# Squared-relu attention and a Fourier mixing layer on one core: blocks of 128 keys instead of 112, other groups of tokens, and a planned order without single corrections

## The chip, the cores and the metric

The kernel runs on one core of a Trainium2 chip. Its metric is the time on the device in microseconds, from one launch; fewer is better. TensorE multiplies matrices, VectorE (DVE) and ScalarE (ACT) do elementwise work, GpSimd (POOL) does some of it and issues the loads that change the type, and SyncE (SP) issues the other transfers, DMA transposes among them.

## The reference

```python
# q, k, v: (8, 12, 448, 64) float32; w_ch1: (768, 3072); w_ch2: (3072, 768)
scores = q @ k.T / sqrt(64)
attn = maximum(scores, 0) ** 2 / 448
x = attn @ v                      # heads side by side: (8, 448, 768)
mixed = real(fft(fft(x, axis=1), axis=2))
u = x + mixed
un = (u - mean(u)) / sqrt(var(u) + 1e-6)
out = u + maximum(un @ w_ch1, 0) @ w_ch2
```

There is no softmax: a block of keys contributes its squared relu times its values, and contributions add up.

## The kernel before

The whole program is written out by a planner (`Streams`) before it runs. Each piece of work is a Python generator that asks for an engine with `need(engine, duration, dependencies, buffers)`; the planner starts, over and over, the piece that could start first by its own estimates, and that fixes the order of instructions on every engine. Engines are strictly in order, so a late operand holds up all that stands behind it. Two tables correct the estimates: `HEAD` moves all pieces of a kind in a phase, and `NUDGE` (line 71) moves one step of one piece. Constants such as `LEAD` (how far attention runs ahead of the feed-forward part) and the margins added to a load's expected landing belong to the same plan.

**Attention.** A batch has 12 heads in three groups of four, a group has two pairs of heads. `load_group` brings q, k and v of a group with one DMA each, with four consecutive tokens on one of 112 partitions: 448 = 112 x 4. For the first two batches `turn_on_pe` transposes q and k on TensorE; later VectorE reorders them (`qkr`, line 539) and a DMA transposes them (`qkT`, line 551). An item of work is one block of 112 keys for a pair of heads: two matmuls of scores (`score`, line 888), each on one half of the array's rows, so that the two run together; a relu on ScalarE out of PSUM (`squares`, line 901); a square on VectorE or ScalarE (`square`, lines 918 and 915); and two matmuls with the values (lines 816 and 873), which again share the array. A pair of heads has four items, a batch 24. After the first batch TensorE visits attention between pieces of the feed-forward part, for up to three items of scores and the values of one pair.

**Mixing.** `fold` and `halves` use the symmetry of the Fourier transform, `mix` multiplies along channels (line 1383), `mix_rows` along tokens, adds x, and normalizes to `un`. Rows of `un` go to DRAM and come back transposed (`turns`), but the first batch and most of the second are turned on TensorE (`turn_rows`, line 1139).

**Feed-forward.** It works on groups of tokens, whose bounds are `GT`: 384, 384 and then eleven of 256. The first layer is line 1870, its relu line 1857. In the second layer a block of 128 tokens is either a whole or half of a `Pair`. A pair (256 tokens, line 2008) needs 84 matmuls of 384 columns where two plain blocks would need 96; it uses sums of weights (`weight_sums`) and sums of hidden blocks made on VectorE. The first group's blocks are plain (line 1898), the second group has a pair and a whole (line 1923), the later ones a pair each. The last four groups are done two at a time (`joint`), with a similar saving in the first layer too.

**Loads.** GpSimd issues them in the order of `loading`: batch 0, q and k of two groups of batch 1, the first weights (`load_w1`), values, then the second weights (`load_w2`) between the groups that follow. For the first three batches at most eight are under way (`ring`).

Of the kernel before, what the change touches and what calls it, by code (L numbers as in the profile page):

```python
# [10 lines left out]
FP32 = mybir.dt.float32  # L11
BF16 = mybir.dt.bfloat16
# [29 lines left out]
class Banks(Bufs):  # L42
# [28 lines left out]
NUDGE = {  # L71
# [6 lines left out]
}  # L78
# [6 lines left out]
class Streams:  # L85
    def __init__(self):
        self.engine = dict.fromkeys(LATENCY, 0.0)
        self.streams = []
        self.fill = lambda: False
        self.port = 0.0  # L90
        self.dma_free = {"sw": 0.0, "hw": 0.0}
        self.count = {}

    def add(self, gen, rank):
        name = gen.gi_code.co_name
        self.count[name] = self.count.get(name, 0) + 1
        self.streams.append([gen, rank, None, name, f"{name}.{self.count[name]}", 0])
# [20 lines left out]
    def run(self):  # L118
        end = {}
        while self.streams:  # L120
            for s in self.streams:
                if s[2] is None:
                    try:
                        s[2] = s[0].send(end.pop(id(s), None))
                        s[5] += 1
# [6 lines left out]
            for s in self.streams:  # L132
# [8 lines left out]
                key = (ok is not None and not ok(), max(t) + HEAD.get((s[3], eng, phase), 0.0) + NUDGE.get((s[4], s[5]), 0.0), s[1][eng != "PE"])  # L141
# [53 lines left out]
def kernel(  # L195
# [34 lines left out]
    WHOLE, FOURTH = 3, 0.1  # L230
    JOINTS = list(range(9, NGR, 2))
# [26 lines left out]
    zero_t = const.tile([128, 1], FP32, name="zero_t")  # L258
    eps_t = const.tile([128, 1], FP32, name="eps_t")
    halfpi = const.tile([128, 1], FP32, name="halfpi")  # L260
# [4 lines left out]
    back = [const.tile([128, 1], mybir.dt.int32, name=f"back{i}") for i in range(2)]  # L265
    back2 = [const.tile([128, 1], mybir.dt.int32, name=f"backe{i}") for i in range(2)]
# [20 lines left out]
    def small_constants():  # L287
# [3 lines left out]
        nc.vector.memset(warm, 0.0)  # L291

    def pads():
        for x in xTc:
# [120 lines left out]
    TURNED, STORED, RELAYED = 1.1055, 1.0, 0.0  # L415
# [13 lines left out]
    def load_group(i, which=(0, 1, 2)):  # L429
# [3 lines left out]
        for x, (nm, src) in enumerate((("q", q), ("k", k), ("v", v))):  # L433
            if x not in which:
                continue
            if b == 0 and x < 2:
                e = yield need("POOL", 0.75, ring())
                t = first_qk[x][:R, g]
            else:
                e = yield need("POOL", 0.75, ring() if b < 3 else [], [BQ[x] if x == 2 else BQ[x][home(i)]])  # L440
                t = work.tile([R, HG, 4 * Dh], BF16, name=f"{nm}n",
                              tag="vn" if x == 2 else f"{nm}n{home(i)}", bufs=3 if x == 2 else 1)
# [1704 lines left out]
```

## Time and profile before

| | us |
|---|---|
| median of 3 runs | 577.06 |
| the runs | 573.18, 577.06, 578.73 |
| the profiled execution, its own time | 574.73 |
| span of that execution in the trace | 572.7 |
| TensorE busy in it | 559.8 |
| VectorE / ScalarE / GpSimd busy | 446.3 / 341.7 / 143.4 |

Groups of instructions are given by line, engine and tile, with their count, the time that they cover and the mean of one in ns. Matmuls overlap: their mean is the time of one from its start to its drain, and the time from start to start is shorter. Timeline rows give the start, the time covered and, in brackets, the idle time before and what ended it. The table of stretches gives, for each, its length, the busy time of each engine with its number of instructions, the clock that TensorE was granted, the busy share of the DMA engines (all queues added up) and the bytes moved.

### The profile page before, as it was taken

The numbers are of one execution on the slowest core, as the hardware profiler recorded it, in microseconds if no ns is written. First come the engines' busy times: TensorE is split into PE (matmuls) and PEld (weight loads), VectorE is DVE, ScalarE is ACT, GpSimd is POOL, SyncE is SP. The second block draws the span as 40 slices with busy tenths as digits, with TensorE's granted clock in tenths as the row PEclk, the third lists the DMA queues.
The fourth block names the chain that finished last, engine by engine and source line by source line (L and its number), as shares of the span: only waits on it lengthen the run. The fifth ranks groups of instructions, "written<-read, shape, count | busy, mean of one in ns | idle before, by whom it ended". The sixth has DMA issues, their size and how long they took to land.

```text
span 572.7 us, 11611 instructions
## 1 busy us (share of the span) xinstructions
PE 559.8 (98%) x4434; PEld 366.5 (64%) x4434; DVE 446.3 (78%) x1030; ACT 341.7 (60%) x573; POOL 143.4 (25%) x193
## 2 busy tenths in 40 slices
PE   8999999899999999999999999999999999999997
PEld 6466556454655846746756756756768688668864
DVE  6988773999797488998998789889899747544843
ACT  5978772789785556877786667748616054106400
POOL 8537101421150111542443225124033000000000
PEclk9999999999999999999999999999999999999999
DMA  9999999697874989599999879934255330322012
GB/s 125 206 211 252 191 225 152 209 133 124 155 181 127 183 103 163 155 177 199 215 158 183 161 124 193 215 106 138 71 131 181 76 104 7 91 96 85 1 44 94
DMA packets 134404, 82.25 MB, mean 144 GB/s; under 512 B 78365, under 2 KB 129566, under 8 KB 134350
## 3 DMA queue, kind: packets, MB, share of 16 engines
q0 software_dynamic: 40384, 33.82, 38.6%
q1 hardware_dynamic: 93966, 47.70, 36.2%
q8 instruction: 34, 0.56, 0.4%
q14 instruction: 20, 0.16, 0.1%
HBM read 62.91 MB, written 26.45 MB: 156 GB/s over the span
## 4 chain that ended last, share of the span: by engine, by line
PE 83%; DVE 8%; DMA 4%; ACT 3%; issue 1%; POOL 1%; DVEq 0%; POOLq 0%; ACTq 0%
PE psF L1870 24%; PE psF L2008 22%; PE psS L1704 7%; PE psS L2008 7%; PE psS L888 6%; PE psF L816 4%; PE psF L1898 3%; PE psF L1704 2%; DMA qkT<-qkr 2%; PE psS L1383 2%; ACT sq L901 2%; DVE sq L918 2%; DMA qk<-in_k_dram 2%; PE psF L1923 1%; PE psS L816 1%
## 5 line engine op out<-in xcount | busy, mean ns | idle before, releaser
L901 ACT ACTIVATE sq<-psS 112x896 bf16<-112x896 f32 x192 | 164.8, 924 | 44.1 <-PE psS L888 43.7
L1870 PE MATMUL psF<-unT,w 128*128 128x256 bf16 (+1 forms) x1296 | 165.8, 285 | 1.0 <-ACT hT L1857 0.7
L1870 PEld LDWEIGHTS <-w 128*128 128x128 bf16 x1296 | 123.6, 98 | 42.4 <-issue 10.8
L918 DVE TENSOR_TENSOR sq<-sq 112x896 bf16<-112x896 bf16 x160 | 98.6, 636 | 9.6 <-ACT sq L901 8.9
L2008 PEld LDWEIGHTS <-hT 128*128 128x128 bf16 x720 | 68.8, 98 | 49.8 <-issue 6.6
L1857 ACT ACTIVATE hT<-psF 128x512 bf16<-128x512 f32 (+3 forms) x136 | 66.2, 504 | 37.9 <-PE psF L1870 37.1
L2008 PE MATMUL psF<-w,hT 128*128 128x384 bf16 x378 | 67.1, 326 | 0.0
L888 PE MATMUL psS<-qkT 64*128 64x448 bf16 (+1 forms) x384 | 52.8, 358 | 3.4 <-DVE qs L1191 1.9
L1568 DVE TENSOR_TENSOR o<-psF,o 128x384 f32<-128x384 f32 x72 | 39.7, 551 | 14.3 <-PE psF L2008 12.6
L888 PEld LDWEIGHTS <-qkT 64*128 64x128 bf16 (+1 forms) x384 | 16.8, 101 | 31.8 <-issue 22.2
L1719 ACT COPY copies<-psS 128x256 f32<-128x256 f32 x51 | 17.8, 374 | 29.0 <-PE psS L1704 26.3
L443 POOL DMA_DIRECT2D qn<-in_q_dram x21 | 15.5, 736 | 73.4 <-DVE qkr L539 73.0
L816 PE MATMUL psF<-sq,vn 112*64 112x448 bf16 x264 | 31.6, 358 | 1.0 <-DVE sq L918 1.0
L443 POOL DMA_DIRECT2D vn<-in_v_dram x24 | 17.3, 722 | 57.6 <-PE psS L888 38.4
L1704 PEld LDWEIGHTS <-w 128*128 128x128 bf16 x288 | 28.1, 98 | 4.3 <-issue 0.2
L1209 POOL TENSOR_TENSOR u<-tp,xn 112x385 f32<-112x385 f32 (+2 forms) x14 | 14.7, 1051 | 62.4 <-DVE tp L1189 60.1
L915 ACT ACTIVATE sq<-sq 112x896 bf16<-112x896 bf16 x32 | 30.1, 955 | 0.3
L642 DVE TENSOR_SCALAR xT<-psF 128x224 bf16<-128x224 f32 x56 | 19.1, 382 | 13.3 <-PE psF L816 13.2
L1218 DVE BATCH_NORM_STATS2 stats<-u 112x6 f32<-112x384 f32 (+2 forms) x56 | 29.1, 545 | 0.3 <-POOL u L1211 0.3
L2008 PE MATMUL psF<-wsum,hT 128*128 128x384 bf16 x162 | 29.0, 326 | 0.0
L816 PEld LDWEIGHTS <-vn 112*64 112x64 bf16 x336 | 15.7, 109 | 19.1 <-issue 12.6
L1568 DVE TENSOR_TENSOR o<-psS,o 128x384 f32<-128x384 f32 x21 | 11.6, 556 | 20.2 <-PE psS L2008 20.2
(233 smaller groups left out, 887.8 us busy)
## 6 DMA issues: line engine op xcount, KB each, us to landing
out_dram<-o SPq DMA_DIRECT2D x56, 192.0 KB, 2.1
vn<-in_v_dram POOLq DMA_DIRECT2D x24, 224.0 KB, 5.8
qn<-in_q_dram POOLq DMA_DIRECT2D x21, 224.0 KB, 5.2
kn<-in_k_dram POOLq DMA_DIRECT2D x21, 224.0 KB, 7.0
w<-in_moe_w_ch_dram POOLq DMA_DIRECT2D x12, 384.0 KB, 13.5
w<-in_moe_w_ch_dram POOLq DMA_DIRECT2D x4, 1152.0 KB, 19.6
utop<-u SPq DMA_DIRECT2D x12, 336.0 KB, 3.1
o<-utop SPq DMA_DIRECT2D x16, 192.0 KB, 5.3
```

Source lines behind the costliest of these rows:

```text
L443: nc.gpsimd.dma_start(out=t, in_=src[b, hs].rearrange("h (p j) d -> p h (j d)", j=4))
L816: nc.tensor.matmul(av[h * Dh:(h + 1) * Dh, 0:S], lhsT=vn[:, c, h0 + h, :], rhs=sq[:, h, :], start=(c == 0), stop=(c == 3))
L888: nc.tensor.matmul(sc[:wide, h, 0:S].rearrange("k (c q) -> k c q", c=4), lhsT=flat[ps, k0:k0 + wide], rhs=qT[ps, m % 2], start=True, stop= ...
L901: nc.scalar.activation(r, sc[:R, :, 0:S], AF.Relu)
L915: nc.scalar.activation(r, r, AF.Square)
L918: nc.vector.tensor_tensor(r, r, r, op=ALU.mult)
L1218: nc.vector.bn_stats(stats[:n, hf, :], u[:n, hf * (D // 2):(hf + 1) * (D // 2)])
L1568: nc.vector.tensor_tensor(o, pc[:, 0:DH], o, op=ALU.add)
L1704: nc.tensor.matmul(ps[:, 0:N], lhsT=lhs, rhs=rhs[:, m], start=(start and m == 0), stop=(stop and m == 2), skip_group_check=True)
L1857: nc.scalar.activation(hs, ps, AF.Relu)
L1870: nc.tensor.matmul(ph[:, i * N:(i + 1) * N], lhsT=w1_sb[m][hf][:, (jj + i) * 128:(jj + i + 1) * 128], rhs=unT[:, m, 0:N], start=(m == 0), ...
L2008: nc.tensor.matmul(pc[:, 0:DH], lhsT=lhs[i], rhs=rhs[i], start=(start and i == 0), stop=(i == KP - 1), skip_group_check=True)
```

## The change

Keys are loaded so that 384 of the 448 of a head lie on 128 partitions, three to each; the last 64 keys of two heads share a fourth block, one head on partitions 0 to 63 and the other on 64 to 127, beside zeros that are written once into homes that stay for k (`kn_homes`) and v (`vn_home`). So a group has seven items for its two pairs instead of eight: six with 128 keys for two heads, and one shared item (`r == 3`), whose two score matmuls use the whole array, one for each pair, and whose values take one matmul for each pair. `load_halves` brings the last 64 keys with two DMAs. The groups of tokens become 384, 512, 384 and nine of 256: the second has a pair and two wholes, the third a pair and a whole, and the fourth weight sum is formed twice. All of batch 1's `un` is now turned on TensorE, and `part_store` goes. The second weights' first quarter is loaded later. `NUDGE` goes with its counting, `HEAD` keeps two entries, and some constants of the plan change. Small tiles (constants, statistics) are put together into larger ones. The cut diff:

```diff
-HEAD = {
-    ('attentions', 'PE', 2): -0.6, ('attentions', 'PE', 3): -0.619, ('chain_b', 'PE', 2): 0.232,
-    ('early', 'DVE', 3): -0.057, ('first', 'DVE', 4): -0.122, ('halves', 'DVE', 1): 0.209,
-    ('halves', 'DVE', 2): -0.148, ('late', 'DVE', 4): -0.128, ('outputs', 'SP', 1): -2.572,
-    ('turn_x', 'SP', 1): 2.085, ('turn_x', 'SP', 2): 0.783, ('turn_x', 'SP', 3): 0.049, ('turns', 'SP', 3): -0.991,
-}
-NUDGE = {
-    ('attentions.1', 45): 0.8, ('attentions.1', 48): 0.28, ('chain_a.1', 4): 0.28, ('chain_a.1', 8): 0.8,
-    ('chain_a.10', 4): -0.13, ('chain_a.11', 8): 0.26, ('chain_b.3', 2): -1.86, ('ffns.1', 123): 0.3,
-    ('ffns.1', 5): -0.53, ('ffns.1', 76): 0.8, ('halves.1', 3): 0.77, ('leave.37', 1): 0.3, ('main.24', 3): -0.3,
-    ('main.7', 6): 0.5, ('mix_rows.7', 3): -1.5, ('rows.12', 4): 0.3, ('rows.14', 3): -0.3, ('rows.23', 2): 1.5,
-    ('rows.9', 2): -1.5, ('squares.75', 1): 0.8, ('third.11', 2): -0.38, ('third.12', 2): -0.8,
-    ('turning.2', 18): 0.26, ('turning.2', 43): 1.7,
-}
+HEAD = {('attentions', 'PE', 2): -0.6, ('attentions', 'PE', 3): -0.6}
...
                 t = [self.engine[eng]] + [d.t if isinstance(d, Cell) else d for d in deps]
                 for p in set(bufs):
                     t.append(sorted(p.free)[bufs.count(p) - 1])
-                key = (ok is not None and not ok(), max(t) + HEAD.get((s[3], eng, phase), 0.0) + NUDGE.get((s[4], s[5]), 0.0), s[1][eng != "PE"])
+                key = (ok is not None and not ok(), max(t) + HEAD.get((s[3], eng, phase), 0.0), s[1][eng != "PE"])
...
+    KB, KT = 128, 3 * 128
+    NB = 7 * NG
...
-    GT = [0, 384] + list(range(768, B * S + 1, 256))
+    GT = [0, 384, 896] + list(range(1280, B * S + 1, 256))
...
-    WHOLE, FOURTH = 3, 0.1
-    JOINTS = list(range(9, NGR, 2))
+    WHOLE = 3
+    JOINTS = list(range(8, NGR, 2))
...
+        clear(nc.vector, first_qk[1].rearrange("p g h x -> p (g h) x")[:, :, 3 * Dh:])
+        clear(nc.vector, vn_home[:, 3 * H * Dh:].rearrange("p (h d) -> p h d", d=Dh))
 
     def pads():
+        for t in kn_homes:
+            clear(nc.gpsimd, t[:, :, 3 * Dh:])
...
+    arrived = {}
+
+    def arrive(i, x):
+
+        arrived.setdefault((i, x), []).append(landed[-1])
+        if len(arrived[i, x]) == (1, 2, 2)[x]:
+            ready[i][x].t = max(arrived[i, x]) + (1.5 if i % NG else 0.0, 3.0, 6.0, 8.0)[min(i // NG, 3)]
+
+    def load_halves(b, g, n, x):
+
+        if b == 0 and x == 1:
+            t = first_qk[1].rearrange("p g h x -> p (g h) x")[:, :, 3 * Dh:]
+        elif x == 1:
+            t = kn_homes[home(b * NG + g)][:, :, 3 * Dh:]
+        else:
+            t = vn_home[:, (3 * H + g * HG) * Dh:(3 * H + (g + n) * HG) * Dh].rearrange("p (h d) -> p h d", d=Dh)
+        for par in range(2):
+            e = yield need("POOL", 0.75, ring() if b < 3 else [])
+            at = (k, v)[x - 1][b, g * HG + par:(g + n) * HG:2, KT:].rearrange("h p d -> p h d")
+            nc.gpsimd.dma_start(out=t[par * Dh:(par + 1) * Dh, par::2], in_=at)
+            landed.append(sch.dma(e, n * HG * Dh * Dh * 2, 390e3, "sw"))
+        for i in range(g, g + n):
+            arrive(b * NG + i, x)
+
+    def load_group(i, which=(0, 1, 2), parts=(0, 1)):
...
+                if x == 0:
+                    to, j, rows = t, 4, S
+                else:
+                    to, j, rows = (t[:, :, 0:3 * Dh] if x == 1 else
+                                   t.rearrange("p (h x) -> p h x", h=HG)), 3, KT
+                nc.gpsimd.dma_start(out=to, in_=src[b, hs, 0:rows].rearrange("h (p j) d -> p h (j d)", j=j))
+                loads[i][x] = None if x == 2 else t.rearrange("p h (j d) -> p j h d", j=4)
+                landed.append(sch.dma(e, GRP * rows / S, 390e3, "sw"))
+                arrive(i, x)
...
+            if x and 1 in parts and (b > 0 or g == x - 1):
+                yield from load_halves(b, g if b else 0, 1 if b else NG, x)
...
+    kn_homes = [work.tile([128, HG, 4 * Dh], BF16, name="kn", tag=f"kn{i}", bufs=1) for i in range(QN)]
+    vn_home = work.tile([128, H * 4 * Dh], BF16, name="vn", tag="vn", bufs=1)
+
+    def clear(eng, t):
+
+        for n in range(2):
+            eng.memset(t[n * Dh:(n + 1) * Dh, 1 - n::2], 0.0)
...
-        yield from load_group(NG, (0, 1))
-        yield from load_group(NG + 1, (0, 1))
+        yield from load_group(NG, (0, 1), (0,))
+        yield from load_group(NG + 1, (0, 1), (0,))
         yield from load_w1(0)
+        yield from load_group(NG, (1,), (1,))
+        yield from load_group(NG + 1, (1,), (1,))
         yield from load_w1(1)
-        yield from load_group(NG, (2,))
-        yield from load_group(NG + 1, (2,))
-        yield from load_w2(range(1))
+        for i in (NG, NG + 1):
+            yield from load_group(i, (2,), (0,))
+        yield from load_halves(1, 0, 2, 2)
         yield from load_group(NG + 2, (0, 1))
-        yield from load_w2(range(1, 2))
+        yield from load_w2(range(2))
         yield from load_group(NG + 2, (2,))
         yield from load_w2(range(2, 4))
...
-                    o = work.tile([R, 4, HG, Dh], BF16, name="qkr", tag=f"qkr{x}", bufs=QR)
+                    o = work.tile([KB if x else R, 4, HG, Dh], BF16, name="qkr", tag=f"qkr{x}", bufs=QR)
...
+    def items(m):
+
+        at = m // 2 * 7
+        return [at, at + 1, at + 2, at + 3] if m % 2 == 0 else [at + 3, at + 4, at + 5, at + 6]
+
+    def past(sets):
+
+        return sets // 2 * 7 + sets % 2 * 3
+
+    def turned_for(b, i):
+
+        g, r = divmod(i, 7)
+        return turned_at[b][g] if r == 3 else [turned_at[b][g][r > 3]]
+
+    def value(av, i, m, sqs, start, stop, e):
+
+        r = i % 7
+        sq, _, home = sqs[i]
+        if r == 3:
+            nc.tensor.matmul(av[:, 0:S], lhsT=vn_home[:, (3 * H + 2 * m) * Dh:(3 * H + 2 * m + 2) * Dh], rhs=sq[:, m % 2, :], start=start, stop=stop,
+                             skip_group_check=True)
+        else:
+            for h in range(2):
+                at = (3 * (2 * m + h) + r % 4) * Dh
+                nc.tensor.matmul(av[h * Dh:(h + 1) * Dh, 0:S], lhsT=vn_home[:, at:at + Dh], rhs=sq[:, h, :],
+                                 start=start, stop=stop, skip_group_check=True)
+        if r != 3 or m % 2:
+            sqs.pop(i)
+            sq_ids.append((e, home))
+            BSQ.free.append(e)
...
     def score(b, i):
 
-        m, c = divmod(i, 4)
-        qT, kT, flat = turned[b][m // 2]
-        wide = R if b < 2 else 128
-        k0 = (2 * c + m % 2) * R
+        g, r = divmod(i, 7)
+        qT, flat, (step, apart) = turned[b][g]
         sc = BS.take()
         for h in range(2):
-            ps = slice(h * Dh, (h + 1) * Dh)
-            nc.tensor.matmul(sc[:wide, h, 0:S].rearrange("k (c q) -> k c q", c=4), lhsT=flat[ps, k0:k0 + wide],
-                             rhs=qT[ps, m % 2], start=True, stop=True)
+            ps = slice(0, 128) if r == 3 else slice(h * Dh, (h + 1) * Dh)
+            pair = h if r == 3 else r // 4
+            k0 = r % 4 * step + pair * apart
+            nc.tensor.matmul(sc[:, h, 0:S].rearrange("k (c q) -> k c q", c=4), lhsT=flat[ps, k0:k0 + KB],
+                             rhs=qT[ps, pair], start=True, stop=True)
         return sc
...
-            r = sqs[i][0] = work.tile([R, 2, S], BF16, name="sq", tag=f"sq{at[1]}", bufs=1)
+            r = sqs[i][0] = work.tile([128, 2, S], BF16, name="sq", tag=f"sq{at[1]}", bufs=1)
             sqs[i][2] = at[1]
-            nc.scalar.activation(r, sc[:R, :, 0:S], AF.Relu)
+            nc.scalar.activation(r, sc[:, :, 0:S], AF.Relu)
...
-            if b == 1 and 2 * ch + i != 1:
-                nr, idn, c0, w = ((128, ident, 64, 128), None,
-                                 (96, ident[:96, :96], 64 + 128, 96), (97, rev[:97, 31:127], 64 + HS, 96))[2 * ch + i]
+            if b == 1:
+                nr, idn, c0, w = ((128, ident, 64, 128), (128, rev[:, 0:127], 64 + HS + 97, 127),
+                                 (96, ident[:96, :96], 64 + 128, 96), (97, rev[:97, 31:128], 64 + HS, 97))[2 * ch + i]
...
-    WHOLES = [[0, 1, 2], [2]] + [[]] * (NGR - 2)
+    WHOLES = [[0, 1, 2], [2, 3], [2]] + [[]] * (NGR - 3)
...
         def fourth():
 
-            kept = JC * 128 // DH
-            yield from several(4, t4, b21, t2, ALU.subtract, [], KP, kept)
+            yield from several(4, t4, b21, t2, ALU.subtract, [])
             yield need("SP", 0.0, [third_done])
-            yield from several(4, t4, b21, t2, ALU.subtract, [], kept)
-
-        sch.add(fourth(), (2, FOURTH))
+            T[4], sums[4].t = None, None
+            yield from several(4, t4, b21, t2, ALU.subtract, [], JC * 128 // DH)
+
+        sch.add(fourth(), (2, 2))
...
-    LEAD, MIXED, SPARE, ELASTIC = 2.7, 1, 0.53, (1, 99)
+    LEAD, MIXED, SPARE, ELASTIC = 2.9, 1, 0.5, (1, 99)
```

More of the change, by code (lines that the diff above doesn't have):

```diff
@@ L456, in load_group @@
                 pads()
[L457 removed]
+            if i == NG + 1 and x == 1 and 0 in parts:
                 yield need("POOL", 3.6)
@@ L562, in turn_on_pe @@
         yield need("PE", 0.0, ready[i][:1] + ([first_scores] if b > 0 else []), [BQT])
-        both = work.tile([128, 2, 8, R], BF16, name="qkT", tag="qkT", bufs=2)
-        turned[b][g] = [both[:, 1 - x].rearrange("q (c r) p -> q r c p", r=2) for x in range(2)]
-        turned[b][g].append(both.rearrange("q x n p -> q (x n p)"))
+        flat = turned_home()[0]
+        pairs = flat.rearrange("q (r x) -> q r x", r=2)
+        turned[b][g] = (pairs[:, :, 4 * KB:].rearrange("q r (c p) -> q r c p", c=4), flat, (KB, 4 * (KB + R)))
         for r in range(2):
@@ L770, in attention @@
             n = min(1 if few else 3, NB - p)
-            ma = pa // 4
+            ma = pv
             lag = 3 if few else 1
             old = fresh[-lag] if len(fresh) >= lag else 0
-            values = pa + 4 <= old if n else True
-            n = max(0, min(n, room - (p - pa - 4 * values)))
+            values = items(pv)[-1] < old if n else True
+            n = max(0, min(n, room - (p - past(pv + values))))
             values = values or not n
@@ L785, in attention @@
             if values:
-                deps += [sv[i][1] for i in range(4 * mv, 4 * mv + 4)]
+                deps += [sv[i][1] for i in items(mv)]
                 if b > 1:
@@ L797, in attention @@
             if n:
-                deps += [turned_at[b][i // 8][i // 4 % 2] for i in (p, p + n - 1)]
+                now = sorted(range(p, p + n), key=lambda i: i % 7 == 3)
+                deps += [c for i in now for c in turned_for(b, i)]
                 bufs += [BS] * n
-                dur += n * mm(S) + SWITCH
+                last = [sum(1 + (j % 7 == 3) for j in now[x + 1:]) * mm(S) for x in range(n)]
+                dur += (n + (now[-1] % 7 == 3)) * mm(S) + SWITCH
             e = yield need("PE", dur + SWITCH, deps, bufs, gate)
@@ L2093 @@
         small_constants()
-        sch.engine.update(POOL=0.5, DVE=0.8)
+        sch.engine.update(POOL=0.5, DVE=2.6)
         sch.add(loading(), (0, 4))
```

214 lines of the change are left out of this document (91 added, 123 removed).

## The prediction

> **What bounds the kernel now.** I read the page first (busy time, DMA, the chain that ended last), then busy time by stage, then the timeline of the stages in which something other than TensorE sets the pace.
>
> ```profile
> span 572.7 us, 11611 instructions
> PE 559.8 (98%) x4434; PEld 366.5 (64%) x4434; DVE 446.3 (78%) x1030; ACT 341.7 (60%) x573; POOL 143.4 (25%) x193
> DMA  9999999697874989599999879934255330322012
> PE 83%; DVE 8%; DMA 4%; ACT 3%; issue 1%; POOL 1%; DVEq 0%; POOLq 0%; ACTq 0%
> ```
>
> ```profile
> core 0: us, PE busy (x) PEld busy (x) DVE busy (x) ACT busy (x) POOL busy (x), PEclk, DMA share, GB/s
> 0.00:52.00 52.00, 47.93 (x525) 31.29 (x526) 42.35 (x105) 40.37 (x63) 29.82 (x70) 1.00 1.13 192
> 52.00:88.00 36.00, 34.48 (x257) 18.27 (x257) 26.43 (x57) 26.47 (x40) 8.64 (x13) 1.00 1.23 215
> 88.00:120.00 32.00, 30.01 (x217) 17.77 (x214) 22.93 (x57) 18.61 (x26) 9.84 (x11) 1.00 1.03 165
> 120.00:240.00 120.00, 119.79 (x897) 72.86 (x896) 97.37 (x221) 86.00 (x145) 26.66 (x32) 1.00 0.81 150
> 240.00:280.00 40.00, 38.97 (x309) 24.21 (x306) 36.95 (x81) 30.54 (x43) 16.96 (x18) 1.00 1.15 181
> 280.00:458.00 178.00, 177.71 (x1402) 119.95 (x1401) 157.59 (x352) 106.57 (x164) 51.44 (x52) 1.00 0.71 148
> 458.00:573.00 115.00, 110.96 (x843) 82.11 (x840) 62.71 (x161) 33.10 (x96) 0.00 (x0) 1.00 0.22 66
> ```
>
> TensorE is the bound, at a granted clock of 1.00. From 120 to 458 us it is idle for 0.21 + 1.03 + 0.29 = 1.53 of 338 us, although VectorE is 81 to 92% busy there: the written order fits this set of operations almost without loss. From 52 to 120 us it idles 1.52 + 1.99 = 3.5 us of 68 (5.2%), while the DMA engines are full (a share above 1 is several queues at once). Before 52 us part of its time is dummy matmuls, and ScalarE and the loads set the pace.
>
> **The blocks of keys.** A batch has 21 items (a block of scores, its relu, its square, its share of the values) where it had 24, so 8 x 3 = 24 of each go.
>
> ```profile
> L901 ACT ACTIVATE sq<-psS 112x896 bf16<-112x896 f32 x192 | 164.8, 924 | 44.1 <-PE psS L888 43.7
> L918 DVE TENSOR_TENSOR sq<-sq 112x896 bf16<-112x896 bf16 x160 | 98.6, 636 | 9.6 <-ACT sq L901 8.9
> ```
>
> Back to back a relu takes 164.8 / 192 = 0.86 us and a square on VectorE 98.6 / 160 = 0.62 us: 20.6 us of ScalarE and at most 14.8 us of VectorE. After 120 us nearly all of that lies beside a full TensorE. What it can give back is bounded by TensorE's idle time from 52 to 120 us: 0 to -3.5. I take -1, since only part of those waits is on the two.
>
> TensorE's own work on the blocks does not shrink. An ordinary item is still a pair of half-array matmuls of 448 columns that run together. The shared block needs two full-array matmuls per four heads for the scores, one after the other, and one per pair for the values: 18 pairs + 6 singles per batch where there were 24 pairs, in both. What goes is one visit of three items per batch, that is its change between the forms.
>
> ```profile
> 71.82 0.78 PE L888 MATMUL psS<-qkT 64*112 64x448 bf16 x6
> 72.53 3.10 PE L1870 MATMUL psF<-unT,w 128*128 128x384 bf16 x18
> 75.56 0.95 PE L816 MATMUL psF<-sq,vn 112*64 112x448 bf16 x8
> ```
>
> From start to start three items take 0.71 us; 18 matmuls of 384 columns take 3.03, so three runs of 448 would take 0.59. A change of form costs about 0.12 us; seven later batches give -0.85.
>
> **The groups of tokens.** From 384, 384, 11 x 256 to 384, 512, 384, 9 x 256; the last four groups, the joints, stay. The 17 blocks of 128 tokens between them were 8 pairs and 1 whole; they become 7 pairs and 3 wholes.
>
> ```profile
> 429.00 15.72 PE psF L1870 x144
> 444.72 13.65 PE psF L2008 x84
> ```
>
> A pair is 84 matmuls of 13.65 / 84 = 0.1625 us; two wholes are 96, so +12 x 0.1625 = +1.95 on TensorE. The first layer keeps its columns. VectorE loses one pair's sums and one addition and forms eight blocks of the fourth weight sum twice, three instructions like these:
>
> ```profile
> L1474 DVE TENSOR_TENSOR w<-w 128x1152 bf16<-128x1152 bf16 x4 | 2.8, 750 | 0.0
> ```
>
> ```profile
> 111.49 0.50 PE L1139 MATMUL psS<-ident,un 128*128 128x128 bf16 x6
> 111.82 3.09 PE L1898 MATMUL psF<-w,hT 128*128 128x384 bf16 x18
> ```
>
> That is 2.3 us under a full TensorE: nothing. All of batch 1 is now turned on TensorE: six more small matmuls, 0.33 us from start to start, +0.3; an indirect store and a one-row store go. The pieces of TensorE's work give -0.85 + 1.95 + 0.3 = +1.4.
>
> **The start.** Two DMAs more for the halves of k and two for v stand ahead of later loads, and a turn of k needs both its parts.
>
> ```profile
> 0.94 0.27 DVE L291 MEMSET warm<- 128x256 uint32 x1
> 3.27 0.96 DVE L353 TENSOR_SCALAR drow<-drow 128x2 f32<-128x2 f32 x1 [2.05 <-POOL drow L278]
> 4.53 0.74 POOL L443 DMA_DIRECT2D vn<-in_v_dram  x1
> 5.26 0.71 POOL L443 DMA_DIRECT2D qk<-in_q_dram  x1
> 7.06 0.39 PE L575 MATMUL psF<-ident,qk 112*64 112x112 bf16 x8
> 9.24 2.54 ACT L901 ACTIVATE sq<-psS 112x896 bf16<-112x896 f32 x3
> ```
>
> ```profile
> 22.86 6.60 ACT L901 ACTIVATE sq<-psS 112x896 bf16<-112x896 f32 x8
> 32.89 1.28 ACT L396 ACT_TABLE_LOAD   x1
> ```
>
> ```profile
> L443 POOL DMA_DIRECT2D kn<-in_k_dram x21: 703/703/759, 10.8 to 353.5; - x21
> DMA to landing us min/median/max: 3.6/5.9/29.4
> ```
>
> The four new clears on VectorE (0.27 us each by the first row) fall into its wait of 2.05 us for GpSimd's indices: nothing, and 1.1 us if that cover were gone. The halves of k take the places of 4.53 and 5.26; with the shortest landing, 3.6, they are there at 8.9, and the first turn of k, at 7.06 now, comes 1.8 us later. Against that, ScalarE works from 9.24 to 32.89 without a pause, and three relus fewer at 6.60 / 8 = 0.825 are -2.5. Net -0.7; between -2.5 (halves hidden) and +3.5 (median landing of 5.9: 4.1 late, little of it made up).
>
> **The loads after that.** Each later group of k or v is one DMA of 384-key rows and two of the halves: four issues more per group, 0.70 us each on GpSimd, 21 x 4 x 0.70 = 59 us on an engine that is 25% busy. Behind an issue that waits for a buffer stand the additions to u and the indirect stores, and behind these VectorE's statistics; from 240 to 280 us, GpSimd's busiest stretch here, it would go from 16.96 of 40 to about 24. That is cover enough, so nothing by itself.
>
> The packets are what I watch: 448 per group become 512 + 256, for the same bytes.
>
> ```profile
> q0 software_dynamic: 40384, 33.82, 38.6%
> q1 hardware_dynamic: 93966, 47.70, 36.2%
> ```
>
> ```profile
> L484 POOL DMA_DIRECT2D w<-in_moe_w_ch_dram x4: 831/851/869, 36.0 to 55.0; - x4
> DMA to landing us min/median/max: 12.4/19.6/26.7
> ```
>
> ```profile
> 86.52 0.43 DVE L539 COPY qkr<-kn 112x1024 bf16<-112x1024 bf16 x1 [0.53 <-DMA kn<-in_k_dram]
> ```
>
> ```profile
> 88.59 3.10 PE L1898 MATMUL psF<-w,hT 128*128 128x384 bf16 x18
> 93.53 2.11 PE L1898 MATMUL psF<-w,hT 128*128 128x384 bf16 x12
> ```
>
> 320 more packets cost nothing if bytes decide. At the mean packet of the hardware queue (36.2% x 572.7 x 16 / 93966 = 35 ns) they cost 0.71 us on 16 engines; at that of the software queue, which carries large rows too, 88 ns and 1.75. Twelve groups of k and v stand ahead of the last quarter of the second weights: 0, 8.5 or 21 us late. That quarter lands at 55.05 + 26.7 = 81.8 at the latest and is needed in the second L1898 row, at 93.53: 11.7 us of slack. Batch 2's k has none: VectorE already waited 0.53 us for it, and behind its copy stand the evictions. TensorE then has two banks of second layer, 48 x 0.1625 = 7.8 us. I take the small-packet row, 8.5 late, since the new rows are smaller still: 8.5 - 7.8 and a little more, +1.5; from 0 to 21 - 7.8 = +13.
>
> [...]
>
> The transposes of k have 128 rows for 112, a seventh more on 18 DMAs; TensorE waits for none of them after 120 us, so nothing. The merged small tiles change no instruction's size: nothing.
>
> **The order.** The 24 nudges of single steps and 11 of 13 offsets go, and the rest of the planner's constants are set anew. The instruction lists follow from a new plan that no run of this page has fitted. Lowest: it stays as tight as 120 to 458 us is, or takes its 1.53 us back. Highest: it idles like 52 to 120 us, 5.2% of 338, +17.4 - 1.5 = +16. Nearest is the least tight stretch with all stages running, 240 to 280: 1.03 of 40, 2.6% of 338 = 8.7, less 1.5: +7.2.
>
> **Sum.** +1.4 (TensorE's work) -0.7 (start) +1.5 (loads) -1 (relief) +7.2 (order) = +8.4 on the profiled execution's 574.73 (span 572.7): 583.1. That execution lies 2.3 below the median 577.06; with half of that added, 584.
>
> **Rivals.**
>
> *Late loads decide (slower still).* The packets cost 1.75 us a group, batch 2's k is 21 us late, VectorE's queue stands at its copy and TensorE runs dry before 120 us: +13 for +1.5, 595. For it: DMA full until 100 us, no slack on that k, the planner's margin for batch 2 cut from 9 to 6 us. Against: equal bytes.
>
> *The relief decides (faster).* The new plan is as tight as the old one. Then halves hidden at the start -2.5, idle time of 52 to 120 us gone -3.5, order -1.5, TensorE's work +1.4: -6.1, 568.6. It decides from where the new order costs under 1 us. For it: VectorE at 92% from 240 to 280 us, just where TensorE idles. Against: that idle time is 1 us, and TensorE's work grows.
>
> *Nothing to be measured.* The order costs 2 to 3 us and the loads nothing: 574.7 + 1.4 - 0.7 - 1 + 2.5 = 577. For it: on a full TensorE small lateness is absorbed by the next group's matmuls. The change doing less than it says is no rival here: the blocks are counted in the loops.
>
> **How the numbers follow.** Forecast 0.46 (its own range 578 to 592), late loads 0.18, relief 0.24, nothing 0.12. About 1% (5.8 us) is what a measurement of this kernel can tell from no change, so the bounds are 571.3 and 582.8. Of the forecast's 0.46 some 0.10 lies below 582.8; slower is 0.36 + 0.18 = 0.54, same 0.10 + 0.12 = 0.22, faster 0.24. The range goes from 567, a little under the relief's sum, to 598, a little over late loads: it leaves out one in ten at each end.
>
> **What would show it.** Right: relus 168, each as long as now; TensorE's work up by about 1 us, its idle time from 120 to 458 us at 5 us or more; the first turn of k near 9 us, the last relu of batch 0 not after 33; the last quarter of the second weights landing near 90. Wrong: idle time from 120 to 458 us still under 3 us (the order was worth nothing), or the second layer starting well after 95 us (packets cost more than I took).

## The result, and the profile after

The changed kernel takes 571.03 us (median of 20 runs, 569.78 to 577.21) beside 576.09 (573.18 to 583.91) of the kernel before: a ratio of 0.9928, 95% interval 0.9905 to 0.9951. It is 0.7% faster. I forecast 584, slower; the range (567 to 598) held the time, the direction was wrong. Medians here and below are of all runs, while the ratios leave out those in a slower state (such as the two at 583.8 and 583.9 of the kernel before), so that medians do not divide exactly to them.

The page of the changed kernel, with the lines that were shown of the kernel before: span, busy time, the software queue, then the relus.

```profile
span 570.5 us, 11231 instructions
PE 557.1 (98%) x4211; PEld 352.0 (62%) x4216; DVE 443.0 (78%) x1028; ACT 315.5 (55%) x526; POOL 195.7 (34%) x279
q0 software_dynamic: 57056, 33.63, 43.8%
L952 ACT ACTIVATE sq<-psS 128x896 bf16<-128x896 f32 x168 | 144.0, 921 | 32.2 <-PE psS L939 31.8
```

And its busy time by the same stages (length, then PE, PEld, DVE, ACT, POOL, clock, DMA share, GB/s):

```profile
52.00:88.00 36.00, 35.24 (x254) 18.08 (x254) 23.01 (x55) 25.23 (x38) 10.64 (x16) 1.00 1.22 189
88.00:120.00 32.00, 30.22 (x213) 18.61 (x213) 24.21 (x57) 14.69 (x21) 15.39 (x20) 1.00 1.19 194
120.00:240.00 120.00, 119.59 (x745) 60.33 (x748) 99.44 (x232) 80.74 (x133) 46.50 (x64) 1.00 0.97 155
240.00:280.00 40.00, 38.90 (x287) 23.57 (x285) 32.47 (x72) 25.42 (x35) 21.42 (x26) 1.00 1.19 182
280.00:458.00 178.00, 177.87 (x1381) 121.26 (x1379) 156.95 (x348) 98.78 (x151) 63.41 (x70) 1.00 0.79 151
```

From 120 to 458 us TensorE idles 0.41 + 1.10 + 0.13 = 1.64 us, where it idled 1.53 before and where I expected 5 or more. A plan without the single delays (the entries of `NUDGE`) runs as tight as the one that was fitted with them. From 52 to 120 us it idles 2.54 us (3.51 before). There are 168 relus, each as long as before.

The feed-forward part starts 2.0 us earlier. The first row is of the kernel before, the second of the changed one:

```profile
51.31 1.15 PE L1870 MATMUL psF<-unT,w 128*128 128x384 bf16 x6
```

```profile
49.30 1.14 PE L1905 MATMUL psF<-unT,w 128*128 128x384 bf16 x6
```

The two profiled executions differ by 2.2 us of span, the medians by 5: before's profiled run was one of its quicker ones (574.73 against 576.09), the changed kernel's one of its slower ones (572.27 against 571.03).

### The profile page after: what moved, and what is told of

Read it like the earlier page. It is cut to its first block, busy times and chain, and to the rows that moved or that the text cites. A ratio compares the mean times of both kernels' runs of the same rounds, so it can differ in the third digit from the quotient of the medians.

```text
span 570.5 us, 11231 instructions
## 1 busy us (share of the span) xinstructions
PE 557.1 (98%) x4211; PEld 352.0 (62%) x4216; DVE 443.0 (78%) x1028; ACT 315.5 (55%) x526; POOL 195.7 (34%) x279
## 3 DMA queue, kind: packets, MB, share of 16 engines
q0 software_dynamic: 57056, 33.63, 43.8%
## 4 chain that ended last, share of the span: by engine, by line
PE 83%; DMA 9%; DVE 4%; POOL 2%; ACT 1%; issue 1%; SPq 0%; DVEq 0%; POOLq 0%; ACTq 0%
PE psF L1905 23%; PE psF L2045 21%; PE psS L1737 8%; PE psS L939 6%; DMA qn<-in_q_dram 6%; PE psS L2045 5%; PE psF L1960 4%; PE psF L812 4%; PE psF L1933 3%; PE psF L1737 2%; PE psS L1417 2%; DVE sq L969 1%; DMA qk<-in_k_dram 1%; DMA kn<-in_k_dram 1%; PE psF L807 1%
## 5 line engine op out<-in xcount | busy, mean ns | idle before, releaser
L1905 PE MATMUL psF<-unT,w 128*128 128x256 bf16 (+2 forms) x1147 | 165.0, 299 | 1.3 <-DVE hT L1890 0.9
L952 ACT ACTIVATE sq<-psS 128x896 bf16<-128x896 f32 x168 | 144.0, 921 | 32.2 <-PE psS L939 31.8
L1905 PEld LDWEIGHTS <-w 128*128 128x128 bf16 x1152 | 110.8, 98 | 50.9 <-issue 6.7
L969 DVE TENSOR_TENSOR sq<-sq 128x896 bf16<-128x896 bf16 x143 | 89.1, 637 | 9.8 <-ACT sq L952 8.9
L1892 ACT ACTIVATE hT<-psF 128x512 bf16<-128x512 f32 (+2 forms) x118 | 58.0, 507 | 42.6 <-PE psF L1905 41.9
L812 PE MATMUL psF<-sq,vn 128*64 128x448 bf16 x246 | 32.7, 362 | 0.4 <-DVE sq L969 0.4
L1737 PEld LDWEIGHTS <-w 128*128 128x128 bf16 x288 | 28.2, 98 | 4.7 <-issue 1.1
L436 POOL DMA_DIRECT2D kn<-in_k_dram x42 | 25.7, 624 | 12.6 <-PE psF L812 7.0
L436 POOL DMA_DIRECT2D vn<-in_v_dram x42 | 26.0, 633 | 9.4 <-DMA w<-in_moe_w_ch_dram 8.2
L461 POOL DMA_DIRECT2D vn<-in_v_dram x24 | 18.9, 787 | 26.9 <-PE psS L939 26.8
L1288 ACT ACTIVATE un<-u,small 113x768 bf16<-113x768 f32 (+2 forms) x21 | 20.9, 1024 | 10.9 <-DVE small L1275 8.3
L812 PEld LDWEIGHTS <-vn 128*64 128x64 bf16 x288 | 12.7, 108 | 21.5 <-issue 17.0
```

Of the source, the lines that this page charges most:

```text
L436: nc.gpsimd.dma_start(out=t[par * Dh:(par + 1) * Dh, par::2], in_=at)
L461: nc.gpsimd.dma_start(out=to, in_=src[b, hs, 0:rows].rearrange("h (p j) d -> p h (j d)", j=j))
L812: nc.tensor.matmul(av[h * Dh:(h + 1) * Dh, 0:S], lhsT=vn_home[:, at:at + Dh], rhs=sq[:, h, :], start=start, stop=stop, skip_group_check=True)
L952: nc.scalar.activation(r, sc[:, :, 0:S], AF.Relu)
L969: nc.vector.tensor_tensor(r, r, r, op=ALU.mult)
L1737: nc.tensor.matmul(ps[:, 0:N], lhsT=lhs, rhs=rhs[:, m], start=(start and m == 0), stop=(stop and m == 2), skip_group_check=True)
```

## Experiments

All ratios are to the kernel before, with 95% intervals.

`SPARE`, `SLACK` and `TURNED` below are further constants of the plan, as `LEAD` and the margins are. "The old structure" is the blocks of 112 keys with the old groups of tokens.

### The order on the old structure

```diff
 old_no_nudges:  -NUDGE = { 24 entries }      +NUDGE = {}
 old_plain:      the same, and HEAD, LEAD, SPARE, SLACK, TURNED
                 and the readiness margins as in the change
```

> The kernel before with NUDGE empty and all else as it was (the 13 offsets of HEAD stay). Theory A, the single delays are worth nothing and a plan without them is as tight: 575 to 578 us, TensorE idle from 120 to 458 us about 1.5 us, as before. Theory B, my prediction's order term, they carry most of 7 us on this structure and the change won that back elsewhere: 581 to 585 us, TensorE idle from 120 to 458 us at 5 us or more.

> The kernel before with NUDGE empty, HEAD cut to the two entries that the change keeps, and the planner's constants of the change (LEAD 2.9, SPARE 0.5, SLACK 0.4, TURNED 1.0, readiness margins 6 and 8 for batches 2 and 3 on): the old blocks and groups in a plan that nobody fitted. Theory A: 575 to 579 us. Theory B: 583 us or more, and then blocks and groups are worth the rest, 12 us or more, down to 571.

Measured: 596.5 us, 1.0365 (1.0317 to 1.0413), and 606.4 us, 1.0563 (1.0539 to 1.0587). The single delays alone are worth 21 us on the old structure, above even the upper end (+16) of my bounds. Theory A has fallen; theory B is right in sign, but what the change won back is far more than 7 us. The stages of old_no_nudges, in the columns of above:

```profile
120.00:240.00 120.00, 113.45 (x803) 65.56 (x800) 100.26 (x228) 79.37 (x134) 27.76 (x32) 0.97 0.81 141
240.00:280.00 40.00, 33.17 (x256) 21.84 (x255) 28.34 (x62) 22.46 (x32) 12.99 (x15) 0.92 1.03 167
280.00:458.00 178.00, 175.58 (x1401) 118.20 (x1400) 162.30 (x353) 109.14 (x163) 50.40 (x53) 1.00 0.72 149
```

TensorE idles 6.55 + 6.83 + 2.42 = 15.8 us there. It is not spread out, and its two longest waits have different causes. Waits of TensorE in old_no_nudges (in total, times, longest):

```profile
PE psF L2001 <- DVE o L1561: 6.9, 2, 6.7
PE psF L1863 <- DMA unT<-ntop: 4.3, 1, 4.3
```

The one of 4.3 us is for the transposed rows of batch 2. The one of 6.7 us, from 268.8 to 275.5, is for an addition on VectorE, which stands in order behind a copy that waits for a DMA transpose of q or k:

```profile
274.57 0.43 DVE L532 COPY qkr<-kn 112x1024 bf16<-112x1024 bf16 x1 [5.41 <-DMA qkT<-qkr]
```

In old_plain, where TensorE idles 26.8 us over the same stages, one row of the timeline holds most of it (its 15.8 is by chance the number of above):

```profile
180.80 0.74 PE L876 MATMUL psS<-qkT 64*128 64x448 bf16 x6
197.33 2.72 PE L1858 MATMUL psF<-unT,w 128*128 128x256 bf16 x12 [15.79 <-DMA unT<-ntop]
```

TensorE waits 15.8 us for the transposed rows of batch 2, which the third group of tokens (768 to 1024) needs. A second wait for such rows, of 5.0 us, comes at 290.

### Which part of the change removes that wait

```diff
 keys_only:    the changed kernel with  GT = [0, 384] + list(range(768, ...))
               and the old wholes, pairs and joints; blocks of 128 keys stay
 groups_only:  old_plain with  GT = [0, 384, 896] + list(range(1280, ...))
               and the new wholes, pairs and joints; blocks of 112 keys stay
```

With the groups go, in both, how batch 1's rows are turned (all of them on TensorE with the new groups) and how the fourth weight sum is formed.

> The changed kernel with the old groups of tokens (384, 384, 256 and so on) put back: blocks of 128 keys, no single delays. If the blocks bring the gain (a start about 2 us shorter, nine visits of attention fewer on TensorE): 570 to 573 us. If the groups bring it (fewer and wider groups, tighter order): 575 us or more. The two wholes in place of a pair that it takes back are 12 matmuls or 1.95 us, so by that term alone it would be 569.

> The old_plain kernel with the new groups (384, 512, 384, 256 and so on), so the old blocks of 112 keys. If the blocks bring the gain: 2 us above old_plain, by the 12 matmuls more. If the groups bring it: several us under old_plain.

Measured: keys_only 599.4 us, 1.0435 (1.0405 to 1.0465); groups_only 584.1 us, 1.0153 (1.0127 to 1.0179). With one set of constants (those of the change), the groups are worth 4.1% with the old blocks and 5.1% with the new (1.0435 to 0.9928); the blocks 1.3% and 2.3%. So the groups, with what goes with them, bring most of it, though by their matmuls they cost 1.95 us. The timeline of keys_only still has the wait:

```profile
188.52 0.74 PE L939 MATMUL psS<-qkT 64*128 64x448 bf16 x6
204.25 2.74 PE L1921 MATMUL psF<-unT,w 128*128 128x256 bf16 x12 [14.99 <-DMA unT<-ntop]
```

Why the groups remove it stands in SyncE's queue beside TensorE's. In the kernel before:

```profile
178.94 2.56 SPq L1324 DMA_TRANSPOSE unT<-ntop  x2
182.40 1.26 SPq L1324 DMA_TRANSPOSE unT<-nbot  x1
```

```profile
183.87 4.31 PE L1870 MATMUL psF<-unT,w 128*128 128x256 bf16 x38
```

In the changed kernel:

```profile
188.53 1.40 SPq L1365 DMA_TRANSPOSE unT<-ntop  x1
194.81 1.26 SPq L1365 DMA_TRANSPOSE unT<-nbot  x1
```

```profile
201.96 3.23 PE L1905 MATMUL psF<-unT,w 128*128 128x384 bf16 x18
```

Before, the last of batch 2's rows are turned at 182.4 and the third group starts 1.5 us after that issue. In old_no_nudges the same turn is issued at 190.75, 8.4 us later, and the group waits: the single delays had brought the rows there just in time. In the changed kernel the last turn is issued 12.4 us later, and it costs nothing, because the second group now holds all the rest of batch 1 (896 = 2 x 448) and the third group starts at 201.96, 18 us later. Some 128 tokens more are done ahead of it: a block of the second layer, 48 x 0.1625 = 7.8 us, and 144 first-layer matmuls with 512 columns for 384, 0.216 us each in the visit shown further below (18 from 146.89 to 150.78) for 0.168 in the prediction's rows, 6.9: an estimate of 15 us.

### The same choice of constants for all four structures

```diff
 old_searched, groups_searched:  LEAD 2.8, SPARE 0.46, SLACK 0.323, one offset
 keys_searched:                  LEAD 3.0, SPARE 0.43, SLACK 0.355, TURNED 1.1, two offsets
 lead_26 (changed kernel):       LEAD 2.6, SPARE 0.64, SLACK 0.331
 spare_59 (changed kernel):      SPARE 0.59, SLACK 0.325
```

> Old blocks and groups, no single delays, constants (LEAD 2.8, SPARE 0.46, SLACK 0.323, one small offset) that give the shortest plan by the kernel's own planner among 160 settings. The same choice for the new structure gave 578 (lead_26) and 576 (spare_59). If the structure is what is faster: 588 us or more, with a gap ahead of batch 2's rows near 190 us. If only the fit counts: 575 to 580.

> New groups, old blocks, constants chosen by the same rule. If the groups carry the robustness: 578 to 584 us and no gap above 3 us near 200 us; if the blocks do: 588 or more.

> New blocks, old groups, constants chosen by the same rule. If the groups carry the robustness: 585 us or more, with the gap ahead of batch 2's rows; if the blocks do: 574 to 580.

> The changed kernel with LEAD 2.6, SPARE 0.64 and SLACK 0.331, a third plan that nobody fitted, with the margins of the change. If the new groups leave slack to plans near this one: 568 to 575 us. If the order of the change is a lucky one: 580 us or more.

> The changed kernel with SPARE 0.59 and SLACK 0.325, a fourth such plan. If the new groups leave slack: 568 to 575 us; if the order is a lucky one: 580 us or more.

The constants of old_searched, groups_searched and keys_searched are those that gave the shortest plan by the planner's own estimate among 160 settings. lead_26 and spare_59 stand for the changed kernel under that rule; no run shows the search itself, and these two change fewer constants than keys_searched does. Measured: old_searched 594.7 us, 1.0309 (1.0283 to 1.0335); keys_searched 594.8, 1.0333 (1.0304 to 1.0362); groups_searched 581.4, 1.0101 (1.0076 to 1.0125); lead_26 578.0, 1.0068 (1.0027 to 1.0110); spare_59 575.6, 0.9995 (0.9964 to 1.0026). So chosen, the groups are worth 2 to 3%, and the blocks nothing with the old groups and 0.3 to 1% with the new ones. lead_26 came out 3 us above the upper end of what I expected, spare_59 0.6 us above it, the others as the structure's theory has it. The wait for batch 2's rows stays in keys_searched (10.8 us) and is in neither lead_26 nor spare_59. So the new structure is worth 2.4% (1.0309 to 1.0068, lead_26) to 3.1% (0.9995, spare_59), and giving up the fit of before costs 3.1% (old_searched): the two roughly cancel. That the changed kernel is 0.7% faster than before, and not level with it, comes with its own constants, to which the next runs turn.

### How far the changed kernel's own constants are a fit

```diff
 old_constants:  LEAD 2.7, SPARE 0.53, SLACK 0.3692, TURNED 1.1055, margins 9 and 5
 margins_only:   margins 9 and 5 alone
 rest_only:      the other four alone
 slack_only:     SLACK 0.3692 alone
 lead_30:        LEAD 3.0 alone
 changed_again:  no edit
```

> The changed kernel with the planner's general constants of before (LEAD 2.7, SPARE 0.53, SLACK 0.3692, TURNED 1.1055, readiness margins 9 and 5), still without single delays. Theory D, the new groups give the order slack (batch 2's rows are first needed after 512 + 384 tokens where it was 384 + 384, some 16 us of TensorE's work later), so that plans near this one are all tight: 568 to 574 us, no gap on TensorE above 3 us. Theory C, the constants that the change set anew are themselves a fit, as the single delays were: 580 us or more, with a long gap somewhere.

> The changed kernel with only the planner's readiness margins of before for loads of batch 2 (9 us) and of batch 3 on (5 us) put back for 6 and 8. old_constants lost 18 us, with gaps at 200 to 217 us, just ahead of batch 2's rows. If the margin of batch 2 is what lost it (the plan puts all of batch 2's work later, and its rows miss the start of the third group): 585 us or more, TensorE starved between 195 and 220 us, and the kernel rest_only stays near 571. If any other constant would do the same, 571 to 575 here.

> The complement of margins_only: LEAD 2.7, SPARE 0.53, SLACK 0.3692, TURNED 1.1055, and the margins of the change. If only the margin counts, 569 to 574 us and no gap above 3 us; if the constants of the change are a fit in all directions, 580 us or more.

> The changed kernel with SLACK 0.3692 (before's value) for 0.4, which moves only the last stage, from some 458 us on. rest_only, which has it too, lost 22 us. If the loss lies ahead of the last stage (its gaps were at 151 to 370 us): 569 to 572 us here, perhaps a little faster than the changed kernel; if SLACK takes part: 575 or more.

> The changed kernel itself, once more, beside the same runs of before as lead_30. If its 571.0 holds on another day: ratio 0.991 to 0.995, and the four neighbours at 575 to 576 are truly slower. If it comes out at 574 to 575 (ratio 0.997 to 1.000), these neighbours cost less than they seem and the gain of the change itself is under 0.5%.

> The changed kernel with LEAD 3.0 for 2.9, the smallest change of the plan that I can make. If plans near this one are as good: 569 to 573 us, perhaps the fastest of all; if the changed kernel's own plan is a lucky one among its neighbours: 575 us or more.

Measured: old_constants 589.8 us, 1.0242 (1.0185 to 1.0299); margins_only 597.2, 1.0380 (1.0321 to 1.0439); rest_only 592.7, 1.0285 (1.0222 to 1.0347); slack_only 575.1, 0.9980 (0.9965 to 0.9995); lead_30 574.1, 0.9982 (0.9947 to 1.0018); changed_again 572.1, 0.9926 (0.9900 to 0.9953). Theory D, that all near plans are tight, has fallen too: all seven plans tried near the change's are slower, so its constants are a fit or a lucky draw (no run tells which), though with fewer numbers than 24 delays. The margins are one lever, but not the only one, since rest_only loses nearly as much, where I had expected 569 to 574 if only the margin counted. The longest of TensorE's waits in margins_only (in total, times, longest):

```profile
PE psF L1905 <- DMA unT<-nbot: 5.5, 1, 5.5
```

The later plan misses the third group again: its last turn of batch 2's rows is issued at 209.4, and TensorE stands from 211.7 to 217.2. That is 5.5 of the 20.5 us that TensorE idles there from 120 to 458 us; the others are shorter waits for VectorE and ScalarE. rest_only has no such wait; its gaps are spread (the longest 2.4 us, for an addition on VectorE). No variant was faster than the changed kernel, whose own time came out the same again.

### Three prices: the form of the array, the relus, the rows

```diff
 single_last:  -sorted(items(mv), key=lambda i: i % 7 != 3)   +... i % 7 == 3
 relus_24:     +for _ in range(2 if b == 0 and i in (5, 12, 19) else 1): relu
 small_rows:   v of batches 1 to 7 in three DMAs with rows of 128 B each
```

> The changed kernel with the full-array matmul of the shared block last among a visit's values, not first. The plan and its instruction counts stay. If a change between full-array and half-array matmuls costs about 0.09 us of TensorE (second layer to second layer 0.163 us, second layer to half-array values 0.256), this adds one such change to about 42 visits: +3 to +4 us over the changed kernel, 574 to 575. If the changes of form hide somewhere: 571.

Measured: 575.9 us, 0.9996 (0.9970 to 1.0023), 4 to 5 us above the changed kernel, about what I expected for a cost that does not hide. One visit of the changed kernel, and the same of single_last:

```profile
143.72 1.69 PE L1905 MATMUL psF<-unT,w 128*128 128x512 bf16 x7
145.24 0.35 PE L807 MATMUL psF<-sq,vn 128*128 128x448 bf16 x1
145.52 0.76 PE L812 MATMUL psF<-sq,vn 128*64 128x448 bf16 x6
146.21 0.74 PE L939 MATMUL psS<-qkT 64*128 64x448 bf16 x6
146.89 4.06 PE L1905 MATMUL psF<-unT,w 128*128 128x512 bf16 x18
150.78 0.35 PE L807 MATMUL psF<-sq,vn 128*128 128x448 bf16 x1
```

```profile
143.82 2.98 PE L1905 MATMUL psF<-unT,w 128*128 128x512 bf16 x13
146.73 0.76 PE L812 MATMUL psF<-sq,vn 128*64 128x448 bf16 x6
147.42 0.36 PE L807 MATMUL psF<-sq,vn 128*128 128x448 bf16 x1
147.71 0.74 PE L939 MATMUL psS<-qkT 64*128 64x448 bf16 x6
```

The full-array matmul L807 keeps TensorE 0.28 us in both places, some 0.09 more than 448 columns take (448 / 512 x 0.216 = 0.19); the next matmul has another form in both. I call that a change of form. Put first, it follows the first layer in the same form and the step into the visit is free: 7 x 0.216 = 1.51 after 143.72 is 145.23. Put last, that step costs 0.1 more (13 x 0.216 = 2.81 after 143.82 is 146.63, not 146.73). The edit reaches the 42 sets of values after the first batch: some 4 us. TensorE's busy time on the page goes from 557.1 to 562.1; 1.3 of these 5.0 us are dummy matmuls (9.1 to 10.4 us), which the edit does not touch.

> The changed kernel with three relus of batch 0 done twice (unplanned, on the same tiles), so 24 relus on ScalarE at the start as before. If ScalarE's chain sets the start, as I took it: the table load and all behind it come 2.5 us later and the time is +2 to +2.5, 573 to 574. If the loads set it: +0 to +0.5.

Measured: 575.1 us, 1.0003 (0.9967 to 1.0040), 3 to 4 us above the changed kernel where I expected 2 to 2.5 if ScalarE's chain sets the start. ScalarE's table load, first in the changed kernel, then in relus_24, and the start of the feed-forward part of relus_24:

```profile
31.27 1.28 ACT L384 ACT_TABLE_LOAD   x1
```

```profile
33.70 1.28 ACT L384 ACT_TABLE_LOAD   x1
51.38 1.14 PE L1906 MATMUL psF<-unT,w 128*128 128x384 bf16 x6
```

2.4 us more on ScalarE become 2.1 us at the feed-forward part and 2.6 at the end of the span (573.1). The three relus of the first batch are the shorter start.

> The changed kernel with each load of v of batches 1 to 7 cut in three DMAs with rows of 128 B where one has rows of 384 B: 1024 packets and two issues of 0.75 us more for each of 21 loads, the same bytes. By the mean packet of the software queue in the changed kernel (43.8% of 16 x 570.5 us by 57056 packets, 70 ns) a load costs 4.5 us more on 16 engines, by the hardware queue's (36 ns) 2.3. If packets are what a load costs, the stage from 52 to 120 us, where the DMA engines are full, gets 9 to 25 us later for the two groups and more of v ahead of the second weights: 577 us or more. If bytes decide: 570 to 573.

Measured: 592.1 us, 1.0284 (1.0230 to 1.0338). The size is as the first theory has it, the way is not: packets were cheap, and GpSimd's issues waited. In the changed kernel's trace an issue that has to wait starts once the DMA issued eight before it has landed: the one at 33.81 follows a landing at 33.53, the one at 39.87 one at 39.59. GpSimd in the changed kernel, then in small_rows, then small_rows' software queue and what TensorE waited for:

```profile
40.53 0.99 POOL L1087 TENSOR_SCALAR un<-u,small 128x768 bf16<-128x768 f32 x1
```

```profile
49.72 0.62 POOL L436 DMA_DIRECT2D vn<-in_v_dram  x1 [2.15 <-DMA w<-in_moe_w_ch_dram]
50.39 2.92 POOL L1090 TENSOR_SCALAR un<-u,small 128x768 bf16<-128x768 f32 x3
```

```profile
q0 software_dynamic: 79232, 33.64, 48.5%
PE psS L1118 <- POOL un L1090: 8.2, 1, 8.2
```

Four issues more for batch 1, 0.74 us each, come behind the first weights, and the waits among these issues grow from 0.42 us in all to 7.8. The normalized rows of batch 0 stand behind them in GpSimd's queue: at 50.39, where the changed kernel has them at 40.53. The packets themselves: 79232 - 57056 = 22176 more took 48.5% of 16 x 591.3 less 43.8% of 16 x 570.5 = 590 us of engine time, 27 ns each.

## Why the prediction was wrong, point by point

**The order (+7.2) is the step that failed.** I priced it as the idle share of the least tight stretch of a fitted plan. That profile holds no unfitted plan, and what an unfitted one costs is not a share: it is single long waits, where rows miss the group that needs them (4.3 us in old_no_nudges) or where VectorE's queue stands behind a transpose (6.7 us). On the old structure it costs 21 us, out of my bounds. On the new one, with the change's own constants, the term came out at 1.64 - 1.53 = 0.1 us. What I did not look for was the slack at the deadlines: that batch 2's rows were turned at 182.4 for a use at 183.9, and that 896 tokens end with a batch, which moves that use by 18 us. I costed the groups by their matmuls alone. And I had put the change down as a plan that nobody had fitted, while all seven neighbours of its constants that were run are slower.

**TensorE's work (+1.4)** was mis-sized. Without the dummy matmuls (10.9 us before, 9.1 after, in the rows below) TensorE's busy time went from 548.9 to 548.0, -0.9. The two wholes for a pair are the 12 matmuls that I said. Mis-sized is the price of a visit: the 0.12 us are the change of form on the way out, and the one on the way in falls on the feed-forward matmul ahead. From 50 us on the traces have 62 visits before and 55 after, as I had it, but 164 and 148 changes of form: 16 changes at 0.09 are some -1.5 us, where I had -0.85. The shared block's entry without a change is no gain over before, since the change comes inside the visit instead (145.24 to 145.52 above); put last it is one change more per visit, which is what single_last shows. The rest of the 2.3 us between +1.4 and -0.9 was not taken apart.

```profile
L2086 PE MATMUL psS<-warm 128*128 128x126 bf16 (+1 forms) x108 | 10.9, 256 | 1.3 <-DVE warm L291 1.3
```

```profile
L2123 PE MATMUL psS<-warm 128*128 128x126 bf16 (+1 forms) x112 | 9.1, 240 | 1.3 <-DVE warm L275 1.3
```

**The start (-0.7)** came out at -2.0. The relus' term (-2.5) was right, as relus_24 shows. The halves of k cost less: their first turn is at 7.46 where I had 8.9, and ScalarE makes up for the later first relu (12.17, 9.24 before): its table load is at 31.27, 32.89 before.

```profile
7.46 0.72 PE L608 MATMUL psF<-ident,qk 128*64 128x128 bf16 x8
```

**The loads (+1.5)** were right in place and near in size (1.7). The last quarter of the second weights lands by 59.6 + 31.9 = 91.5 (I had 90), and batch 2's q and k are what is late: VectorE stands 5.37 us at its copy, the eviction L1436 behind it, and TensorE loses 1.7.

```profile
L511 POOL DMA_DIRECT2D w<-in_moe_w_ch_dram x4: 826/841/856, 53.1 to 59.6; - x4
DMA to landing us min/median/max: 17.8/26.0/31.9
```

```profile
94.37 0.43 DVE L568 COPY qkr<-qn 112x1024 bf16<-112x1024 bf16 x1 [5.37 <-DMA qn<-in_q_dram]
PE psS L1229 <- DVE pc L1436: 1.7, 1, 1.7
```

The 16672 packets more of the software queue took 43.8% of 16 x 570.5 less 38.6% of 16 x 572.7 = 461 us, 28 ns each, 0.55 us a group where I took 0.71. In the changed kernel's trace the packets of this queue take 73 ns at 512 B, 60 at 384 and 35 at 128 in the mean: the shorter, the less time.

**The relief (-1)** was too small. Idle time from 52 to 120 us fell from 3.51 to 2.54 us, but 1.7 of the 2.54 is the wait for the loads, counted above; of the old waits 0.8 is left, -2.7. How much of that is the fewer items was not tested.

These terms overlap (the start is read at the feed-forward part, the work over the whole span), so they do not add up to the 2.2 us of span. The rival that came true, the relief at 568.6, was right to say that it decides where the order costs under 1 us. Its own sum is near 571 in part by luck: it took -1.5 for the order, which came out at +0.1, and -3.5 for the idle time up to 120 us, which came out at -1.0, against +1.4 for TensorE's work, which came out at -0.9.

Open: why other constants cost 3 to 26 us has been followed for the margins alone, and there for one of several waits; for `SLACK`, `LEAD` and the rest it was not followed. The old delays were not tried on the new structure, whose pieces they do not name.

## What to carry to other kernels

In a kernel whose order is written out, look for the deadlines before pricing a change of the order: for each group of work, when its last operand is ready and when it is first used. A slack of 1.5 us that single corrections hold is a debt; a group bound moved onto a batch bound put the use 18 us later, more than any instruction count in the change. The bound does not make every plan tight: with other margins the rows miss it again. And a plan's tightness is a property of plan and structure together: take away the corrections on the old structure first, or both effects hide in one small sum.

## What the runs showed of the hardware

Long waits on TensorE cost more than their length in old_plain and old_no_nudges. After the 15.8 us of old_plain the granted clock is 0.50 and then 0.75 over two stretches of 2 us, and only then 1.00; after the 4.3 us of old_no_nudges it is 0.50 for the 4 us that are shown and 0.56 in the mean of the next 2, then 1.00.

```profile
181.00:197.00 16.00, 0.54 (x6) 0.10 (x2) 6.33 (x18) 5.91 (x8) 7.09 (x8) 0.67 1.00 176
197.00:199.00 2.00, 1.67 (x9) 1.20 (x10) 0.00 (x0) 0.00 (x0) 0.00 (x0) 0.50 0.65 129
199.00:201.00 2.00, 2.00 (x15) 0.93 (x15) 0.03 (x1) 0.60 (x1) 0.00 (x0) 0.75 0.00 0
201.00:203.00 2.00, 2.00 (x20) 1.42 (x17) 1.97 (x5) 1.73 (x3) 0.00 (x0) 1.00 0.04 9
```

```profile
188.30:192.60 4.30, 0.01 (x2) 0.00 (x0) 1.13 (x3) 2.21 (x3) 0.34 (x1) 0.88 1.36 228
192.60:194.60 2.00, 1.98 (x10) 1.43 (x11) 0.00 (x0) 0.00 (x0) 0.00 (x0) 0.50 1.29 204
194.60:196.60 2.00, 2.00 (x11) 1.42 (x10) 1.21 (x3) 0.00 (x0) 0.00 (x0) 0.50 1.05 268
```

The stretches at 1.00 begin 3.7 us after the wait of 15.8 us has ended (at 197.33) and 6.0 us after that of 4.3 (at 192.6). In old_plain 12 first-layer matmuls of 256 columns cover 2.72 us from 197.33, and 24 of them 2.79 us from 201.53. The lower clock is most of why old_no_nudges, with the matmuls of the kernel before, has TensorE busy for 567.5 us and not 559.8: by the clocks after its two long waits (after the one of 6.7 us the clock is 0.50 for 4 us and 0.84 in the mean of the next 2.5), an estimate, some 5 of the 7.7 us.
